# A new common order for 2,210 operations of a gated linear attention with a mixer behind it

## The chip, the cores and the metric

The kernel runs on one core of a Trainium2 chip. The metric is the device time of one execution in microseconds; the time before is 555.85 us, the median of 3 runs (555.32 to 556.29). The profile is one further execution taken by the hardware profiler, on core 0, whose span from the first to the last instruction is 552.8 us.

## The reference

The first half is a gated recurrence with complex gates per head (4 batches, 8 heads, 768 steps, 48 channels), the second a mixer on its result.

```python
scale = np.minimum(mag, 0.999) / (mag + 1e-06)
a_re_n, a_im_n = (a_re * scale, a_im * scale)
for t in range(S):
    new_re = ar * S_re - ai * S_im
    new_im = ar * S_im + ai * S_re
    S_re, S_im = (new_re + kv, new_im)
    y[:, :, t] = np.einsum('bhd,bhde->bhe', q[:, :, t], S_re)
...
h = xt @ U @ V
u = x + h.transpose(0, 2, 1)
ch = np.maximum(u @ w_ch1, 0.0) @ w_ch2
return (u + ch).astype(np.float32)
```

All arrays are float32 apart from the weights of the mixer, which arrive as float64 words and are narrowed on the chip.

## The kernel before, in words

**Tiles and stages.** A batch of 768 steps is cut into 6 chunks of 128, so there are 24 chunks; two chunks make a group (12 groups, for the gates) and two make a block of the mixer (12 blocks, m = 0 to 11). For a group, the gates are loaded (`load_a`), their magnitudes and logarithms are worked out on ScalarE and VectorE (`magnitudes_of`), summed along time by a matmul and exponentiated (`within`, tile `es`), and their angles are summed by a matmul and rounded (`angles`, tile `F`; L764 is VectorE's part, L758, L755 and L761 are the matmuls) and turned into cosine and sine (`waves_of`, tile `cs`). The decay over a whole chunk is the last row of `es`; it is stored to DRAM (`TD<-es`, L706) and loaded back turned (`T<-TD`, L709). For a chunk, q and k are loaded (L548) and v (L550), weighed by `es` and multiplied by `cs` on VectorE (`prep`, tile `QKC`), transposed on TensorE (L816) and copied by ScalarE (L822); then come the products inside the chunk (`inner`, L845), the state (`dk`, L865, and `G`), and the outputs (`y`, L894 and L902). The mixer runs over blocks: a low-rank mix (L960), a transpose (L976), the up product and the down product. Block 0 uses plain up products (L991); blocks from 2 on use products with fewer multiplications (`few`, L1103) and the down product in a Strassen-like form (`down_two`, L1235, whose sums on VectorE are L1227 and whose additions to the result are L444). For that form w2 is changed in place once, for block 1 (`w2_of(0, 1)` becomes a difference, L1305).

**Narrowing the weights.** w1 arrives in six loads and w2 in six more (`stage<-in_moe_w_ch_dram`, L569), each followed by five steps on VectorE, or three there and two on ScalarE (`single`, L582 to L588).

**The order.** The kernel does not issue its instructions where they are written. Every step is added to a `Plan` as a numbered operation with its engine, what it reads and what it writes. `ORDER` is a tuple of all 2,210 numbers: the operations are issued in this common order, and so each engine's own queue is the tuple filtered by engine (SyncE 192 operations, VectorE 793, ScalarE 553, TensorE 624, GpSimd 48). An engine works through its queue strictly in order: an operation that has to wait holds up everything behind it on the same engine. Reads and writes given to `add` are used in `Plan.order` alone, for an assertion that no operation comes before what it needs and that no buffer is taken too early; the real waits are put in from the tiles that the instructions touch. Buffers in PSUM are given out in the order of the tuple as well.

**Fillers.** `SPARE` says ahead of which operation how many extra products of the identity with itself are issued (`idle`, L1387 and L1383); they write the buffer that the operation is about to take, and nothing reads them.

**The range count.** At the end a count of gates outside the range of this method (`judge`, tiles `bad`, `least`, `flag`) decides whether a slow general path runs. All engines load the flag (L1395) after their last work of the main path.

**Forms on TensorE.** Its operations differ in how they divide the array: whole (up, few, down), in halves of rows (`inner`, `y` L902), in quarters (`dk`, `y` L894), in row strips that are transposed (`tr`, `mixed`), and the corrections of block 0.

Of the kernel before, what the change touches and what calls it, by code (L numbers as in the profile page):

```python
# [114 lines left out]
)  # L115

SPARE = {
    125: 2, 135: 10, 199: 14, 209: 1, 223: 5, 243: 2,
}

DUMP = None
# [195 lines left out]
def kernel(  # L317
# [19 lines left out]
    DM = H * D  # L337
# [580 lines left out]
    def mixer(m, ahead=False):  # L918
# [281 lines left out]
        def down_two():  # L1200
# [29 lines left out]
            def product(to, part, x, y, reads, first=True):  # L1230
# [6 lines left out]
                for half in range(2):  # L1237
                    PE(0.975, RM, lambda half=half: products(half), reads(half) + [("w2s", 0)],
                       [to + (part,), ("bank", to[1])], steps=KH)
# [215 lines left out]
```

## Time and profile before

| | us |
|---|---|
| median of the runs | 555.85 |
| span of the profiled execution | 552.8 |
| TensorE busy | 526.9 |
| VectorE busy | 432.8 |
| ScalarE busy | 317.8 |
| GpSimd busy | 32.2 |
| first matmul starts | 11.04 |
| last addition on VectorE starts | 548.02 |

An operation's row gives its start, its length, engine and line, what is written from what, and in brackets how long the engine had been idle and who ended that. Several operations of one kind in a row are merged. PEld is the loading of weights into the array, which overlaps the products. A "place" is an operation's position in its engine's own queue, counted from 0 in the tuple; it comes from the code and not from the trace. "Work ahead" of an operation is the time of all operations before it in its queue, without waits.

### The profile page before, as it was taken

What the parts mean: (1) busy time and instruction counts of PE and PEld (TensorE: products, weight loads), DVE (VectorE), ACT (ScalarE), POOL (GpSimd) and SP (SyncE); (2) the same over time, 40 slices, a digit from 0 to 9 for tenths busy, and PEclk for the clock granted to TensorE, in tenths of its full rate; (3) what the DMA queues carried; (4) which work ended last, traced back from release to release, by engine and by line L of the source; (5) the groups of instructions that cost most, each with busy time, mean ns of one, the idle gap of its engine ahead of it and who ended that gap; (6) DMA issues with size and microseconds to landing.
All of it is one profiled execution on the core that took longest, in us unless ns stands there. A gap on an engine that the chain in (4) does not pass through costs nothing.

```text
span 552.8 us, 16672 instructions
## 1 busy us (share of the span) xinstructions
PE 526.9 (95%) x7228; PEld 477.3 (86%) x7228; DVE 432.8 (78%) x828; ACT 317.8 (57%) x553; POOL 32.2 (6%) x61
## 2 busy tenths in 40 slices
PE   2899999999999999999999999999999999999996
PEld 1677776767999987999999998999999989999995
DVE  6899989999999987998787987786953635567352
ACT  6889999795597787567827956626512232110100
POOL 1000000001010000102001001002000000000000
PEclk9999999999999999999999999999999999999999
DMA  9988876523441354314513425003300000000001
GB/s 229 187 184 174 195 170 151 144 30 87 88 89 30 56 104 77 59 31 85 91 38 67 74 38 111 2 1 59 59 9 23 17 11 15 8 8 23 21 9 34
DMA packets 150688, 39.92 MB, mean 72 GB/s; under 512 B 145912, under 2 KB 147408, under 8 KB 150608
## 3 DMA queue, kind: packets, MB, share of 16 engines
q1 hardware_dynamic: 148400, 34.43, 31.2%
q0 software_dynamic: 2208, 4.35, 2.3%
q8 instruction: 59, 0.97, 0.7%
q14 instruction: 21, 0.17, 0.1%
HBM read 33.60 MB, written 4.76 MB: 69 GB/s over the span
## 4 chain that ended last, share of the span: by engine, by line
PE 73%; DVE 12%; ACT 4%; issue 2%; DMA 1%; POOL 0%; DVEq 0%; SPq 0%; ACTq 0%; POOLq 0%
PE down L1235 26%; PE few L1103 25%; PE tr L816 4%; PE dk L865 3%; PE inner L845 3%; PE y L902 3%; PE up L991 2%; PE y L894 2%; DVE xo L444 1%; ACT gate L438 1%; PE rank L937 1%; PE ph L755 1%; PE mixed L960 1%; PE uTp L976 1%; PE es ps L691 1%
## 5 line engine op out<-in xcount | busy, mean ns | idle before, releaser
L1111 ACT COPY h<-few 128x512 f32<-128x512 f32 x60 | 35.1, 585 | 87.3 <-PE few L1103 87.1
L1235 PE MATMUL down<-w,h 128*128 128x192 f32 x396 | 72.7, 330 | 0.9 <-DVE xo L444 0.7
L438 ACT ACTIVATE gate<-gate 128x768 f32<-128x768 f32 (+2 forms) x74 | 65.6, 900 | 9.2 <-DVE GS L750 3.8
L1235 PEld LDWEIGHTS down<-w,h 128*128 128x128 f32 x396 | 64.5, 190 | 3.7 <-issue 1.5
L822 ACT COPY QK<-tr 112x512 f32<-112x512 f32 x96 | 49.9, 596 | 17.8 <-PE tr L816 17.7
L444 DVE TENSOR_TENSOR xo<-down,xo 128x192 f32<-128x192 f32 (+1 forms) x79 | 29.9, 385 | 33.9 <-PE down L1235 33.4
L1115 DVE CUSTOM_DVE_ANT_1 h<-few,h 128x512 f32<-128x512 f32 x60 | 40.5, 686 | 15.7 <-PE few L1103 11.8
L1103 PE MATMUL few<-extra,w 128*128 128x128 f32 x400 | 50.9, 276 | 0.0
L1103 PEld LDWEIGHTS few<-extra,w 128*128 128x128 f32 x400 | 48.0, 192 | 0.1
L441 DVE TENSOR_TENSOR QKC<-qk,cs 128x768 f32<-128x768 f32 x48 | 44.4, 950 | 1.7 <-PE dk L865 1.3
L1235 PE MATMUL down<-stage 128*128 128x192 f32 x198 | 37.9, 330 | 0.4 <-DVE xo L444 0.4
L438 ACT ACTIVATE es<-es ps 128x384 f32<-128x384 f32 x48 | 20.1, 502 | 31.2 <-PE es ps L691 29.2
L444 DVE TENSOR_TENSOR h<-few,h 128x512 f32<-128x512 f32 x30 | 20.6, 688 | 20.4 <-ACT h L1111 12.1
L1179 POOL DMA_DIRECT2D out_dram<-xo x32 | 17.9, 558 | 313.8 <-DVE xo L444 297.7
L991 PE MATMUL up<-uT,w 128*128 128x256 f32 x144 | 34.5, 387 | 0.7 <-ACT uT L980 0.7
L1235 PEld LDWEIGHTS down<-stage 128*128 128x128 f32 x198 | 32.3, 190 | 1.7 <-DVE xo L444 1.0
L1103 PE MATMUL few<-gate,w 128*128 128x128 f32 x240 | 32.2, 278 | 0.4 <-DVE gate L1075 0.4
L435 ACT ACT_TABLE_LOAD x24 | 30.8, 1283 | 1.1 <-PEq L1439 0.7
L816 PEld LDWEIGHTS tr<-ident,QKC 64*112 64x112 f32 x768 | 24.2, 130 | 8.3 <-issue 3.6
L816 PE MATMUL tr<-ident,QKC 64*112 64x64 f32 x768 | 28.9, 221 | 2.4 <-DVE QKC L441 2.4
L991 PEld LDWEIGHTS up<-uT,w 128*128 128x128 f32 x144 | 26.4, 190 | 5.3 <-ACT uT L980 0.9
L1103 PEld LDWEIGHTS few<-gate,w 128*128 128x128 f32 x240 | 29.3, 192 | 0.8 <-PE uTp L976 0.6
(161 smaller groups left out, 1100.4 us busy)
## 6 DMA issues: line engine op xcount, KB each, us to landing
stage<-in_moe_w_ch_dram SPq DMA_DIRECT2D x12, 768.0 KB
gate<-in_a_im_dram SPq DMA_DIRECT2D x24, 192.0 KB
gate<-in_a_re_dram SPq DMA_DIRECT2D x24, 192.0 KB
VP<-in_v_dram SPq DMA_DIRECT2D x24, 192.0 KB
qk<-in_q_dram SPq DMA_DIRECT2D x24, 192.0 KB
qk<-in_k_dram SPq DMA_DIRECT2D x24, 192.0 KB
out_dram<-xo POOLq DMA_DIRECT2D x12, 192.0 KB, 2.2
out_dram<-xo POOLq DMA_DIRECT2D x20, 96.0 KB, 2.1
```

Of the source, the lines that this page charges most:

```text
L435: ACT(1.4, rank, lambda: nc.scalar.preload_act_table_set(name), writes=[TABLE])
L438: return nc.scalar.activation(out=o, in_=i, func=f, **kw)
L441: nc.vector.tensor_tensor(out=o, in0=a, in1=b, op=OP.mult)
L444: nc.vector.tensor_tensor(out=o, in0=a, in1=b, op=OP.add)
L816: nc.tensor.transpose(out=get(*ps[r])[0:DQ, h], in_=get(*qkc)[at, h].rearrange("p u d -> p (u d)")[:, 0:DQ], identity=ident[at, at], tile_ ...
L822: nc.scalar.copy(out=get(*QK)[:, u].rearrange("p (h t) -> p h t", t=CH)[:, :, r * HC:(r + 1) * HC], in_=get(*ps[r])[0:DQ])
L991: nc.tensor.matmul(out=get(*ps)[:, e], lhsT=w1[:, f, (ff + e) * 128:(ff + e + 1) * 128], rhs=get(*uT)[:, f], start=(f == 0), stop=(f == KD ...
L1103: nc.tensor.matmul(out=get(*ps)[:, q], lhsT=w()[:, q * 128:(q + 1) * 128], rhs=v[0](), start=(n == 0 and q == 0), stop=True, skip_group_ch ...
L1111: ACT(c_act(n3 * CH) - 0.045, RU, lambda i=i, k=k: nc.scalar.copy(out=at(i, k), in_=get(*ps)), [ps], [o])
L1115: DVE(c_dve(n3 * CH), RU, lambda i=i, k=k: nc.vector._custom_dve(dve_ops.TENSOR_ADD_SAT, out=at(i, k), in0=get(*ps), in1=at(i, k), s0=math ...
L1179: queue.dma_start(out=out[b, c * CH:(c + 1) * CH, lo:hi], in_=get("xo", i)[:, lo:hi])
L1235: nc.tensor.matmul(out=get(*to)[:, part], lhsT=x(j), rhs=y[:, j], start=(first and j == 0), stop=(j == KH - 1), skip_group_check=not first)
```

## The change

The tuple `ORDER` is replaced as a whole, with the same 2,210 numbers in another sequence. Four operations have other reads or writes, and one filler of 34 is left out, the one ahead of operation 209, a state product of chunk 0.

```diff
 ORDER = (
-    95, 93, 91, 0, 92, 94, 196, 150, 5, 96, 99, 11, 3, 100, 4, 151, 97, 152, 101, 98, 149, 112, 115, 194, 116, 106, 218, 113, 102, 195, 107, 114, 117,
...
-    2188, 2182, 2178, 2185, 2183, 2189, 2199, 2184, 2192, 2190, 2186, 2193, 2187, 2191, 2195, 2194, 2200, 2196, 2201, 2197, 2198, 2202, 2203,
+    91, 95, 93, 99, 96, 97, 98, 101, 102, 92, 94, 100, 112, 104, 115, 106, 0, 5, 103, 113, 114, 117, 118, 105, 116, 119, 120, 6, 121, 3, 109, 107,
...
+    2182, 2178, 2188, 2185, 2184, 2183, 2175, 2192, 2186, 2187, 2190, 2193, 2195, 2199, 2194, 2189, 2200, 2196, 2191, 2197, 2198, 2121, 2125, 2201,
+    2202, 2203, 1710,
 )
 SPARE = {
-    125: 2, 135: 10, 199: 14, 209: 1, 223: 5, 243: 2,
+    125: 2, 135: 10, 199: 14, 223: 5, 243: 2,
 }
...
-                                                                     in_=get(*y[1])[side(r, 1)]), [y[1] + (r,)], [xi + (r + 1,)])
+                                                                     in_=get(*y[1])[side(r, 1)]), [y[1]], [xi + (r + 1,)])
...
-                    PE(0.975, RM, lambda half=half: products(half), reads(half) + [("w2s", 0)],
+                    PE(0.975, RM, lambda half=half: products(half), reads(half) + [("w2s", 0), ("w2i", 0)],
...
-                DVE(c_dve(DH if y is not None else DM), R0, f, [ps + (part,)] + ([] if also is None else [ps + (also,)]),
+                DVE(c_dve(DH if y is not None else DM), R0, f, [ps + (part,), ("bank", ps[1])] + ([] if also is None else [ps + (also,)]),
...
-                                                                    op=OP.subtract), [("w2s", 0)], ALL_W2)
+                                                                    op=OP.subtract), [("w2s", 0)], ALL_W2 + [("w2i", 0)])
```

What the sequence becomes for the operations that matter below, as places in the engine's own queue:

| operation (number) | engine | place before | place after |
|---|---|---|---|
| load of w1's first block (5) | SyncE | 7 | 5 |
| load of v of chunk 0 (196) | SyncE | 5 | 15 |
| store of es(1), group 0's decay (129) | SyncE | 25 | 11 |
| loads T<-TD of group 0 (130, 131) | SyncE | 31, 32 | 26, 24 |
| stores of es(2), es(3) (173, 174) | SyncE | 36, 37 | 33, 30 |
| loads of q, k of chunk 2 (265, 266) | SyncE | 30, 29 | 34, 31 |
| stores of es(4), es(5) (339, 340) | SyncE | 55, 57 | 45, 48 |
| first widening step of w1 block 0 (6) | VectorE | 15 | 11 |
| gate product with a_im, chunk 0 (108) | VectorE | 9 | 18 |
| F of chunk 0 (137) | VectorE | 22 | 23 |
| w1 block 1, first four steps (12, 14, 13, 15) | VectorE | 20, 21, 18, 23 | 19, 20, 21, 22 |
| F of chunk 3 (187) | VectorE | 63 | 60 |
| weighing of q, k of chunk 2 (268) | VectorE | 49 | 62 |
| transposes of chunk 4's second half (369) | TensorE | 59 | 58 |
| up block (0, 8), second product (260) | TensorE | 53 | 61 |
| inner products of chunk 2 (277) | TensorE | 38 | 42 |
| product of the range count (2208) | TensorE | 439 | 589 |
| cast of the flag (2209) | VectorE | 610 | 780 |
| store of block 8's second half (1710) | GpSimd | 41 | 47 |

164 rows, old and new, of the table ORDER are left out of this document.

## The prediction

> **What bounds the kernel now.** I read the page first, then the busy time by stretch, then what TensorE waited for.
>
> ```profile
> span 552.8 us, 16672 instructions
> PE 526.9 (95%) x7228; PEld 477.3 (86%) x7228; DVE 432.8 (78%) x828; ACT 317.8 (57%) x553; POOL 32.2 (6%) x61
> ```
>
> ```profile
> 0.00:44.00 44.00, 29.32 (x463) 22.63 (x464) 37.96 (x77) 34.47 (x61) 2.17 (x14) 1.00 0.97 201
> 44.00:80.00 36.00, 33.97 (x651) 27.43 (x649) 35.97 (x58) 33.79 (x59) 0.00 (x0) 1.00 0.82 177
> 80.00:200.00 120.00, 118.96 (x1653) 99.60 (x1649) 113.17 (x200) 94.97 (x158) 8.37 (x12) 1.00 0.42 90
> 200.00:300.00 100.00, 97.85 (x1407) 91.39 (x1406) 86.40 (x171) 68.16 (x118) 7.70 (x12) 1.00 0.35 66
> 300.00:400.00 100.00, 99.43 (x1476) 94.04 (x1476) 81.63 (x164) 59.84 (x109) 7.42 (x11) 1.00 0.24 47
> 400.00:500.00 100.00, 99.83 (x1279) 95.58 (x1272) 53.16 (x110) 22.13 (x47) 3.82 (x7) 1.00 0.05 14
> 500.00:548.00 48.00, 47.57 (x338) 46.62 (x336) 24.16 (x51) 4.41 (x8) 2.69 (x5) 1.00 0.05 18
> ```
>
> The columns are the stretch, its length, then busy time of PE, PEld, DVE, ACT, POOL, the granted clock, the DMA share and GB/s. From 44 us on TensorE stands still for 2.03 + 1.04 + 2.15 + 0.57 + 0.17 + 0.43 = 6.4 us in all. No order of the same products can take more than that out of these 504 us. The other reserve lies before 44 us: 14.7 us of TensorE idle, and fillers that only pass time. VectorE is as full as TensorE up to 80 us (35.97 of 36), so the early part is a race of two engines: TensorE follows VectorE at a distance, and this distance is never caught up later, because afterwards TensorE has work without a break.
>
> ```profile
> 71.00 1.83 DVE L441 TENSOR_TENSOR QKC<-qk,cs 128x768 f32<-128x768 f32 x2
> 72.98 0.66 PE L816 MATMUL tr<-ident,QKC 64*112 64x64 f32 x16 [0.53 <-DVE QKC L441]
> 23.58 0.95 DVE L654 CUSTOM_DVE_ANT_0 GL<-gate 128x768 f32<-128x768 f32 x1
> 24.45 1.82 DVE L441 TENSOR_TENSOR QKC<-qk,cs 128x768 f32<-128x768 f32 x2
> ```
>
> The first two rows show the distance at work: the transposes of chunk 4's second half start 0.15 us after VectorE's product, having waited for it. The other two give the unit in which I count: an operation of 0.95 us takes 0.87 of its queue (23.58 to 24.45). Counted like this, start to next start where nothing waits, the old order has 64.4 us of VectorE work up to the end of that product and 44.6 us of TensorE work ahead of the transposes. So VectorE has lost 72.83 - 64.4 = 8.4 us up to there, TensorE 72.98 - 44.6 = 28.4, and the step demands a lag of 64.4 - 44.6 = 19.8 us. Over all TensorE steps of the old order the largest such lag is 20.0 (the second product of up block (0, 8), which needs w1's last block), and 8.4 + 20.0 is the 28.4 seen. Above this the end adds 28.4 to 35 us of loss, which is the 6.4 us of idle.
>
> **The change, part by part.** The four edits of reads and writes (whole `y[1]`, `("w2i", 0)`, `("bank", ...)`) add names to a list that is only asserted against the order; they emit no instruction, so 0 us. What runs is the new tuple.
>
> *VectorE's own loss, first 40 us.*
>
> ```profile
> 5.04 0.56 DVE L657 CUSTOM_DVE_ANT_0 low<-gate 128x384 f32<-128x384 f32 x1 [2.40 <-DMA gate<-in_a_re_dram]
> 11.66 0.56 DVE L444 TENSOR_TENSOR GL<-GL,gate 128x384 f32<-128x384 f32 x1 [0.46 <-ACT gate L438]
> 19.16 0.55 DVE L764 SCALAR_TENSOR_TENSOR F<-F,ph 128x384 f32<-128x384 f32 x1 [1.54 <-ACT F L438]
> 18.55 0.58 ACT L438 ACTIVATE F<-ph,magic 128x384 f32<-128x384 f32 x1 [0.59 <-PE ph L758]
> ```
>
> Of the 8.4 us lost, 5.04 is the first landing, which stays; 0.46 and 1.54 are two waits. The new queue puts the first widening step of w1 in front of the 11.66 operation, and all four steps of w1's block 1 plus the product `gate * a_im` of chunk 0 between it and the 19.16 one. These fill the 2.0 us. ScalarE's copy of `prefix_z` and its steps of chunk 0 shift too, so that by the same durations the F of chunk 0 is ready about 1.0 us sooner than 18.55 + 0.58. Walking through the new queues with the trace's durations, chunk 0's QKC starts at 22.6 and not 24.45, a gain of 1.85. But F of chunk 3 (old place 63, new 60) comes too early by some 1.1 us, as its phase sum follows on TensorE and ScalarE. So I take 0.75. Bounds: 0 (every gain waits elsewhere) and 2.0.
>
> *The lag.* In the new tuple the same transposes have 42.8 us of TensorE and 60.3 us of VectorE work ahead, a lag of 17.5; the largest of all steps is 18.2 (inner products of chunk 2). VectorE's deferred work is what changed: the second product of up block (0, 8) stands 8 places later, and the weighing of chunk 2's q and k 13 later. 20.0 - 18.2 = 1.8 us. Bounds: 0, where ScalarE or a transfer is met first, and 1.8. Together 2.55.
>
> *Changes of form.* TensorE's operations differ in how they split the array; where the form changes, the same work takes longer.
>
> ```profile
> 180.66 1.09 PE few L1103 x8
> 192.98 1.17 PE down L1235 x6
> 251.99 0.89 PE few L1103 x8
> 252.88 0.98 PE down L1235 x6
> ```
>
> These rows are of the chain of waits: alone among others of their kind 0.89 and 0.98, beside a step of another form 1.09 and 1.17, 0.2 more. The old order has 160 such changes, the new 150. By the most 10 x 0.2 = 2.0 us; but which forms meet changes also (from quarter to full fewer, from row to full more), and the sum of every step's usual time in its own neighbourhood is 512.4 us against 512.0. I take 0.4; bounds -0.5 (the mix costs more) and 2.0.
>
> *Tail.*
>
> ```profile
> 539.74 0.36 DVE L444 TENSOR_TENSOR xo<-down,xo 128x192 f32<-128x192 f32 x1 [0.62 <-PE down L1235]
> 540.48 0.35 DVE L444 TENSOR_TENSOR xo<-down,xo 128x192 f32<-128x192 f32 x1
> 540.89 1.24 PE L1235 MATMUL down<-stage 128*128 128x192 f32 x6 [0.21 <-DVE xo L444]
> L1377 DVE CAST flag<-bad ps x1: 136/136/136, 389.3 to 389.3; 1x1 int32<-1x1 f32 x1
> L1395 PEldq TENSOR_LOAD <-flag x1: 487/487/487, 544.9 to 544.9; - x1
> L1395 ACTq TENSOR_LOAD <-flag x1: 462/462/462, 526.5 to 526.5; - x1
> ```
>
> The last 14 TensorE steps are the same in both. On VectorE a sum of h (0.47) no longer stands between the two additions at 539.74 and 540.48, so the 0.21 us of waiting goes, with some of the change of form beside it: 0.3, bounds 0 and 0.4. The flag is not made earlier but later: its cast moves from VectorE's place 610 to 780 of 793, near 534 us. ScalarE reads the flag once its own work is done, at 526.5, and would wait, but nothing is queued behind it; TensorE reads at 544.9, 10 us later than the cast. So 0.
>
> *The filler* left out is these two:
>
> ```profile
> 26.04 0.46 PE L1387 MATMUL dk<-ident 128*128 128x96 f32 x2
> ```
>
> It lies where TensorE waits for VectorE anyway: 0, and 0.4 at most if that cover went.
>
> *From 80 us on* I keep the remaining 4.4 us of idle (1.04 + 2.15 + 0.57 + 0.17 + 0.43). The trace shows no wait of the new order; bounds are 2.4 less, as the lag that steps near 200 us demand falls from some 7 to 8 us to 4 to 5 in the new tuple, and 4 more.
>
> Sum: 0.75 + 1.8 + 0.4 + 0.3 = 3.25 us. The profiled span is 552.8 and the median of the runs 555.85, 3.05 outside the span; I leave that as it is: span 549.6, median 552.6.
>
> **The rivals.**
>
> *SyncE's queue gets in the way: slower.*
>
> ```profile
> 15.38 2.02 SPq L548 DMA_DIRECT2D qk<-in_k_dram  x2
> 24.61 0.38 SPq L706 DMA_DIRECT2D TD<-es  x1
> 27.02 1.00 SPq L548 DMA_DIRECT2D qk<-in_q_dram  x1
> 28.13 5.41 SPq L709 DMA_DIRECT2D T<-TD  x2
> 22.71 0.95 DVE L441 TENSOR_TENSOR qk<-qk,es 128x768 f32<-128x768 f32 x1
> 37.38 0.95 DVE L441 TENSOR_TENSOR qk<-qk,es 128x768 f32<-128x768 f32 x1
> ```
>
> SyncE waits in order. The store of es(1) moves from place 25 to 11, ahead of chunk 0's and 1's q and k; group 1's stores move to places 30 and 33, around chunk 2's. Chunk 0's k was through at 17.40 and used at 22.71, so a load needs 5.3 us at most. In the new queue es(1) is ready near 14, when SyncE gets there, and costs about 1; chunk 2's last half goes out near 36.5 instead of 27.02, behind es(3), and VectorE wants it near 44.9 (place 62, no longer 37.38). 36.5 + 1 + 5.3 = 42.8: 2.1 us to spare. If the slow pair T<-TD (5.41) comes in between, it is 3.3 late, VectorE stands, and TensorE with it. The same pattern returns at group 2 (stores at places 45 and 48 ahead of q and k of chunk 5). One such hit takes back the whole gain, two give 552.6 + 6.6 = 559.2. It decides once chunk 2's last half is issued after 44.9 - 5.3 = 39.6. Against it: after 80 us all but three of the new queue's loads have over 6 us of TensorE work between what releases them and what uses them.
>
> *The gain is hidden anyway: no change.* The idle of 2.15 us at 200 to 300 shows that something else sets TensorE's pace there. If TensorE, being earlier, waits that much more: 2.55 of 3.25 lost, 555.2. For it: VectorE lost time for TensorE there as well (86.40 of 100). Against: the smaller lags named above.
>
> *More gain.* The later idle shrinks by the 2.4 of the bounds and VectorE's 2.0 come whole: 552.6 - 2.4 - 1.2 = 549.0.
>
> *A colder start.*
>
> ```profile
> 11.04 1.62 PE L695 MATMUL es ps<-GL,prefix_r 128*128 128x384 f32 x2 [11.04 <-DVE GL L444]
> 13.30 1.49 PE L695 MATMUL es ps<-GL,prefix_r 128*128 128x384 f32 x2
> 33.93 0.91 PE L695 MATMUL es ps<-GL,prefix_r 128*128 128x384 f32 x2
> ```
>
> The first two pairs take 0.6 to 0.7 us more than a later one. If the steps to 20 us (three of this size) stayed that slow because TensorE begins about 1 us sooner, that is 3 x 0.65 = 2.0: 554.6. [...]
>
> **How the numbers follow.** Forecast 0.52, more gain 0.17, slower by the queue 0.19, no change 0.09, colder start 0.03. A run of this kernel tells 0.2% (1.1 us) from no change: faster is below 554.7, slower above 557.0. Faster is 0.52 + 0.17 + half of the colder start = 0.70; same 0.09 + the other half = 0.11; slower 0.19. Predicted is 552.6. The largest gains together are 2.0 + 1.8 + 2.0 + 0.4 + 2.4 = 8.6, 547.3; that all come at once is unlikely, so the range begins at 547.8. With no gain early, 0.5 lost on forms and 4 more of idle it would be 552.6 + 2.55 + 0.9 + 4 = 560.0; the range ends at 557.6, between one hit and two of the queue, and leaves the rest out. The forecast's own range is 550.5 to 554.3.
>
> **What would show it.** Right: chunk 0's QKC on VectorE near 22.6; the first transposes near 23.6 instead of 25.45; chunk 4's, after 42.8 us of work and 25.9 of loss, near 68.7; about 2.5 us less TensorE loss at 80 us, and TensorE idle from 80 us on still near 4.4; no 0.21 in the tail. Wrong: VectorE waiting for a transfer of q or k before 60 us, T<-TD in front of it on SyncE; or TensorE idle over 7 us after 80 us; or products longer by more changes of form.

## The result, and the profile after

The changed kernel takes 548.01 us (median of 4 runs, 547.12 to 550.12) against 556.07 us for the kernel before in the same comparison: ratio 0.986, 95% interval 0.9838 to 0.9883. That is 8.1 us less, where 3.25 were forecast. The profiled execution spans 545.8 us, 7.0 less than the one of before.

The first lines of the page of the changed kernel, and its busy time by the stretches that were shown of before (stretch, length, then PE, PEld, DVE, ACT, POOL, granted clock, DMA share, GB/s):

```profile
span 545.8 us, 16645 instructions
PE 522.9 (96%) x7226; PEld 475.8 (87%) x7226; DVE 433.5 (79%) x828; ACT 316.2 (58%) x553; POOL 31.9 (6%) x61
```

```profile
0.00:44.00 44.00, 29.30 (x464) 22.92 (x465) 38.84 (x79) 36.16 (x64) 2.03 (x14) 1.00 0.87 184
44.00:80.00 36.00, 33.26 (x647) 27.05 (x646) 32.99 (x49) 33.60 (x59) 0.00 (x0) 1.00 0.80 180
80.00:200.00 120.00, 119.56 (x1666) 100.01 (x1665) 115.27 (x200) 95.15 (x156) 7.88 (x11) 0.99 0.46 95
200.00:300.00 100.00, 99.94 (x1456) 94.43 (x1454) 88.23 (x173) 65.86 (x116) 7.60 (x12) 1.00 0.32 61
300.00:400.00 100.00, 100.00 (x1431) 95.36 (x1430) 77.94 (x153) 57.02 (x102) 7.58 (x12) 1.00 0.27 50
400.00:500.00 100.00, 100.00 (x1284) 95.78 (x1283) 58.89 (x129) 24.95 (x53) 3.56 (x7) 1.00 0.06 15
500.00:541.00 41.00, 40.86 (x291) 40.27 (x289) 21.09 (x50) 3.51 (x6) 3.21 (x6) 1.00 0.07 24
```

TensorE's idle time behind 44 us is 2.74 + 0.44 + 0.06 + 0 + 0 + 0.14 = 3.4 us, 3.0 less than before. From 80 us on it has almost gone (0.64 against 4.4); from 44 to 80 us it has grown by 0.7. TensorE's busy time over the whole execution fell too, from 526.9 to 522.9 us, with the same products but for one filler of less than 0.5 us.

Idle time alone therefore does not show where the time went. TensorE runs the same 624 steps in both kernels, and at some points of its queue exactly the same set of steps is done in both traces. The time at which the next step starts can be compared there without any model:

| steps done | before, us | changed, us | difference |
|---|---|---|---|
| 6 | 26.43 | 24.80 | -1.63 |
| 28 | 45.03 | 43.65 | -1.38 |
| 43 | 59.05 | 58.12 | -0.93 |
| 83 | 91.42 | 91.88 | +0.47 |
| 117 | 129.54 | 130.17 | +0.63 |
| 187 | 187.44 | 187.22 | -0.22 |
| 289 | 268.13 | 265.72 | -2.41 |
| 324 | 296.28 | 292.40 | -3.87 |
| 590 | 515.17 | 508.61 | -6.56 |
| 616 | 539.54 | 532.89 | -6.65 |
| 623 | 546.84 | 539.72 | -7.12 |

So an early lead of about 1 us is won, lost again between 59 and 92 us, and the whole gain is made from 130 us on, bit by bit: 0.85 to 187 us, 2.2 to 268, 1.5 to 296, 2.7 to 515, and 0.6 behind that.

What eats the early lead stands in TensorE's rows around 78 us:

```profile
22.93 1.82 DVE L442 TENSOR_TENSOR QKC<-qk,cs 128x768 f32<-128x768 f32 x2
23.94 0.66 PE L817 MATMUL tr<-ident,QKC 64*112 64x64 f32 x16 [0.78 <-DVE QKC L442]
69.92 1.12 PE L817 MATMUL tr<-ident,QKC 64*112 64x64 f32 x32 [0.61 <-DVE QKC L442]
74.80 2.36 PE L866 MATMUL dk<-VP,QKC 64*64 64x48 f32 x96
77.09 1.15 PE L846 MATMUL inner<-QK 112*64 112x64 f32 x31
80.01 1.98 PE L846 MATMUL inner<-QK 112*64 112x64 f32 x33 [1.77 <-issue]
81.92 0.87 PE L938 MATMUL rank<-xo,UV 128*32 128x384 f32 x4
```

```profile
76.50:80.00 3.50, 1.74 (x54) 1.55 (x50) 1.76 (x4) 3.50 (x6) 0.00 (x0) 1.00 0.71 205
80.00:83.40 3.40, 3.39 (x45) 2.04 (x44) 2.54 (x4) 2.56 (x4) 0.00 (x0) 0.50 0.02 5
83.40:87.00 3.60, 3.60 (x135) 3.44 (x132) 3.50 (x6) 1.35 (x3) 0.00 (x0) 1.00 0.31 46
```

The first transposes come at 23.94 and not 25.45, those of chunk 4 at 69.92 and not 72.98. Then follow 96 products of the state (two passes of 48) and the inner products of chunks 4 and 5 without a long operation in between, and in the middle of the inner products TensorE stands still for 1.77 us. This standstill is called the hole below. "issue" says that TensorE waited for nothing that the profile shows. In the window behind this hole the granted clock (the eighth column) is 0.50: the 33 inner products take 1.98 us there, and the rank products behind them 1.44 instead of 0.78 to their next step. Compared with the same steps at full clock (the loads experiment below) the half clock costs 0.83 + 0.66 = 1.5 us, the hole 1.77.

Instructions come to the core by DMA too. The page lists their queue with packets, MB and share of 16 engines:

```profile
q8 instruction: 59, 0.97, 0.8%
```

0.97 MB in 59 packets is 16,384 bytes each, and the trace has the time of every packet. TensorE's 14,551 instructions (products, weight loads and the few that only wait) make 247 for each of the 59 packets. In the changed kernel one of these packets lands from 68.33 to 69.70 us, the next only from 77.64 to 78.61, after 439 TensorE instructions; TensorE resumes 1.40 us after its end.

### The profile page after: what moved, and what is told of

The parts are those of the page before. It is cut to its first block, busy times and chain, and to the rows that moved or that the text cites. A ratio compares the mean times of both kernels' runs of the same rounds, so it can differ in the third digit from the quotient of the medians.

```text
span 545.8 us, 16645 instructions
## 1 busy us (share of the span) xinstructions
PE 522.9 (96%) x7226; PEld 475.8 (87%) x7226; DVE 433.5 (79%) x828; ACT 316.2 (58%) x553; POOL 31.9 (6%) x61
## 3 DMA queue, kind: packets, MB, share of 16 engines
q0 software_dynamic: 2208, 4.35, 2.4%
## 4 chain that ended last, share of the span: by engine, by line
PE 87%; DVE 5%; ACT 3%; DMA 2%; issue 1%; SPq 1%; DVEq 0%; ACTq 0%
PE down L1236 29%; PE few L1104 25%; PE inner L846 4%; PE up L992 4%; PE tr L817 4%; PE dk L866 4%; PE y L903 4%; PE y L895 2%; DMA gate<-in_a_im_dram 2%; PE rank L938 2%; PE mixed L961 2%; PE uTp L977 1%; PE es ps L692 1%; ACT gate L439 1%; PE ph L756 1%
## 5 line engine op out<-in xcount | busy, mean ns | idle before, releaser
L823 ACT COPY QK<-tr 112x512 f32<-112x512 f32 x96 | 51.1, 595 | 34.8 <-PE tr L817 34.6
L742 POOL DMA_DIRECT2D gate<-F x15 | 12.2, 810 | 324.3 <-DVE F L765 170.6
L817 PE MATMUL tr<-ident,QKC 64*112 64x64 f32 x768 | 27.4, 219 | 2.9 <-DVE QKC L442 2.9
L1180 POOL DMA_DIRECT2D out_dram<-xo x32 | 20.2, 681 | 168.1 <-issue 86.1
```

The lines of the kernel that those rows point to most:

```text
L817: nc.tensor.transpose(out=get(*ps[r])[0:DQ, h], in_=get(*qkc)[at, h].rearrange("p u d -> p (u d)")[:, 0:DQ], identity=ident[at, at], tile_ ...
L823: nc.scalar.copy(out=get(*QK)[:, u].rearrange("p (h t) -> p h t", t=CH)[:, :, r * HC:(r + 1) * HC], in_=get(*ps[r])[0:DQ])
```

## The experiments

Two things had to be settled: where the gain is made, and what the hole is. Theory A said that the gain is made behind 130 us and the early lead is given back; theory B that the early lead is the cause and the later waits vanish because of it. Theory F said that the hole is TensorE waiting for its own instructions; theory G that it is a hidden wait for another engine. Further theories are named in the expectations. Ratios are to the kernel before, run beside each experiment (medians 555.3 to 556.3 us). Where a diff lists a few numbers, it is a piece of one engine's queue. A "seam" is where a run goes over from one sequence to the other.

### One part of the order at a time

The first run has the new sequence early and the old one late, the second the reverse, cut after 600 numbers.

```diff
 ORDER = (
-    (before) all 2210 numbers in the old sequence
+    the first 600 of the new sequence, the others as in the old one
```

> The first 600 numbers of the new tuple (up to about 130 us of TensorE's work, with the filler left out), then all others in the old sequence. Theory A (the gain is made behind 130 us, where the new queues leave TensorE almost no waits; what is won before 80 us is given back by 100 us): ratio to the kernel before 0.996 to 1.003, TensorE idle behind 130 us near the old 4 us. Theory B (the early lead is the gain, and because TensorE and VectorE are in better step the later waits vanish of themselves): ratio 0.986 to 0.990, TensorE idle behind 130 us near 0.5 us.

564.93 us, ratio 1.0153 (1.0124 to 1.0182): slower by 8.7 us, which neither theory had. The hole at 78 us was there (2.80 us, half clock behind it), and at the seam TensorE stood for 1.54 us, waiting for ScalarE, and for 4.54, waiting for VectorE, with 6.8 us at half clock behind that. These take more than any early lead could give, so the run tells little of theory B.

```diff
 ORDER = (
-    (before) all 2210 numbers in the old sequence
+    the first 600 of the old sequence, the others as in the new one
```

> The first 600 numbers of the old tuple, then all others in the new sequence, the filler kept. Theory A (the gain is made behind 130 us): ratio 0.986 to 0.990, TensorE idle behind 130 us below 1 us. Theory B (the early lead is the gain): ratio 0.997 to 1.002.

549.94 us, ratio 0.991 (0.9879 to 0.9941): 6.3 us less without any of the new early order. Behind 200 us TensorE's idle time is 0.3 us (0.2 in the changed kernel). The seam cost 0.78 us at 139, and a hole of 1.67 us stood at 198; with these two the ratio is just above the range of theory A, and far from that of theory B.

The first run was repeated with the cut at one time on all engines (what the changed kernel's trace starts before 115 us).

```diff
 ORDER = (
-    the first 600 of the new sequence, the others as in the old one
+    what the new order starts before 115 us, the others as in the old one
```

> The new sequence for all operations that the changed kernel's trace starts before 115 us, the old sequence for all others (the seam is at one time on all engines, which it was not in the first run of this kind). Theory A (early gain of 1 to 3 us, given back by the hole at 78 us and the half clock behind it): ratio 0.999 to 1.006. Theory B (the early lead lets the later waits vanish): ratio 0.986 to 0.991. If the hole stays away by chance: ratio 0.993 to 0.998.

560.55 us, ratio 1.0096 (1.0078 to 1.0115). Again slower, outside all three ranges. The profiled execution is the longest of the seven (566.93 us), so its trace shows more than the median lost: the hole of 2.58 us at 77 us with 13.6 us at half clock behind it, and at 134 us a wait of 3.61 us for VectorE, with 6.8 us more at half clock:

```profile
137.32 0.69 PE L756 MATMUL ph<-GS,prefix_r 128*128 128x384 f32 x1 [3.61 <-DVE GS L750]
```

At 120 us VectorE has worked 108.6 us in the changed kernel's trace and 110.0 in that of before, so it comes later to the seam than the old queues behind it expect. What decides against theory B is the stretch behind the seam: the run is 11.8 us behind the kernel before after 125 steps and 12.1 at the end, and the first run 9.8 after 140 steps and 9.9 at the end. The old late queues gain nothing there. And in the changed kernel itself no lead is left after 83 steps, ahead of the whole gain.

Two further runs measured the late part. The first changes the order only for what the old one starts from 288 us on, the second is the late part of above with the last correction of the loads (below), which takes most of the hole at 198 us away.

```diff
 ORDER = (
-    (before) all 2210 numbers in the old sequence
+    what the old order starts before 288 us, the others as in the new one
```

> The old order for all operations that the trace of before starts until 288 us, the new sequence for all others. Theory S (the late gain comes bit by bit, wherever the new queues of all engines leave TensorE slack): behind 288 us the old order loses some 5.5 us to TensorE's rate and the new one 2.5, so 2 to 3.5 us less: ratio 0.9935 to 0.9965. Theory T (the gain needs the state that the new order has built up before 288 us): less than 1 us, ratio 0.998 to 1.002.

552.75 us, ratio 0.9938 (0.9915 to 0.9962). In its trace TensorE is 1.66 us behind the kernel before after 312 steps (a half clock at 26 to 30 us, which the trace of before does not have) and 1.59 ahead at the end: 3.25 us gained behind 288 us, as theory S expected.

> The first 600 numbers of the old tuple as in e2_late_new, then the sequence of e13_loads3, so without the hole of 1.7 us that e2_late_new had at 198 us. Theory A (the gain is made behind 130 us): ratio 0.986 to 0.990, 1 to 2 us less than e2_late_new, and what e13_loads3 has beyond that is the early part without its hole, 2 to 4 us. If the early part is worth nothing even without its hole, e13_loads3 and this run are within 1 us.

549.39 us, ratio 0.9887 (0.9863 to 0.9911). Theory A holds in its main point; the hole at 198 us shrank to 0.90 us only. The second half of the expectation missed: the run with the corrected loads and the new early part (543.52 us, below) is 5.9 us faster than this one, where 2 to 4 were expected. So the early part is worth something once its hole is smaller: in the traces that run is 2.9 us ahead of this one after 105 steps, 3.9 after 136 (behind the seam), 5.0 after 208 (behind the hole) and 6.4 at the end. Why the last 1.4 us come is open.

A count shows what the late part has that the old one lacks. For every TensorE step the traces give the time between the end of the last operation of another engine that it needs (an input, or the emptying of its bank of PSUM) and its own start. Steps with less than 0.3 us (how inputs and banks are counted moves an entry by up to 2):

| stretch, us | before | changed | new only behind 288 us |
|---|---|---|---|
| 200 to 300 | 23 | 11 | 23 |
| 300 to 400 | 26 | 15 | 16 |
| 400 to 500 | 23 | 11 | 11 |
| 500 to end | 8 | 3 | 3 |

There are some 80 of these tight steps in the old order and some 40 in the new one. The run with the new order behind 288 us has the old count ahead of it and the new one behind it. An estimate from the two traces says how much of the gain they carry. The usual time from one step's start to the next is the median over the same pair of kinds of step, both with more than 0.5 us to spare, behind 80 us in both traces. Behind 130 us the intervals that begin or end with a tight step exceed it by 6.9 us in the old order and by 1.7 in the new one, which is 5.2 of some 7 us gained there; all other intervals exceed it by 3.4 and 1.4. No run took the tight steps out by themselves, so this is worked out and not tested.

### Can single waits be taken out of the old order?

If the late waits are local, moving a few operations of ScalarE forward should do. Theory L says that they are; theory H says that the next wait takes their place. Here are the rows of before, at 198 us, that the first move was made for:

```profile
197.63 1.12 PE L845 MATMUL inner<-QK 112*64 112x64 f32 x32
198.04 1.49 ACT L438 ACTIVATE gate<-gate 128x1536 f32<-128x1536 f32 x1 [1.07 <-DVE GS L750]
199.56 0.64 ACT L913 COPY xo<-y 64x192 f32<-64x192 f32 x2
200.22 0.32 ACT L911 COPY xo<-y 128x192 f32<-128x192 f32 x1
200.86 0.78 PE L865 MATMUL dk<-VP,QKC 64*48 64x48 f32 x21 [0.47 <-issue]
```

The three copies empty two banks; their data was there at 197.80. They stand behind a gate step of 1.49 us which itself had waited 1.07 for VectorE, so the second bank was free only at 200.54. The move took TensorE's 0.7 us at 200.86 for a wait for it (0.47 of them show as idle; the rest lies in products that the trace books as busy). The program and the trace say otherwise. The steps that take these two banks start at 202.51 and 205.04, long after. The idle time lies inside a step, behind 11 of its 16 products, where no wait for another engine stands, and it ends 1.50 us after an instruction packet (198.39 to 199.36). It is a smaller hole of the kind at 78 us.

```diff
 ORDER = (
-    1178, 836, 837, 835,
+    837, 1178, 836, 835,
...
-    1817, 1476,
+    1476, 1817,
...
-    646, 455,
+    455, 646,
...
-    406, 405, 407,
+    407, 406, 405,
```

> The old order with ten operations of ScalarE at other places of its queue and nothing else changed: the copies 836, 837, 835 ahead of the gate step 1178, the activation 1476 ahead of the gate step 1817, 455 ahead of the gate step 646, 407 ahead of 406. Theory L (the old order's waits behind 80 us are local, each a small operation of ScalarE or VectorE that frees a bank and stands behind a long one, and TensorE sets the pace): the waits of 0.70, 0.68, 0.59 and 0.52 us vanish and the time falls by 1.2 to 2.5 us, ratio 0.9945 to 0.998. Theory H (something else sets the pace there, so that the next wait takes it up): ratio 0.998 to 1.002.

556.1 us, ratio 1.0016 (1.0005 to 1.0028). Of the three copies only one (837) came ahead of the gate step, other than the expectation says. TensorE's queue is the same in both, so the two traces can be subtracted step by step. At 200 us 0.85 us are won, after 0.61 had been lost just before: TensorE waits for ScalarE there (0.31 us of it idle), comes later to the end of its instruction block, and the hole is gone. That tells nothing of a wait for a bank. At 344 us 0.44 are won and 0.83 + 0.64 lost: the gate step 1817 now waits for 1476 and ends at 345.55 instead of 343.51, and the copies of chunk 19 and an addition of VectorE, which TensorE needs, stand behind it. Only 0.44 of the loss comes back in the 200 us that follow. At this place the wait is real, as theory L has it, and the next one takes its place, as theory H has it.

```diff
 ORDER = (
-    1817, 1476, 1794, 1793, 1797, 1798,
+    1476, 1794, 1793, 1797, 1798, 1817,
...
-    1178, 836, 837, 835,
+    837, 1178, 836, 835,
...
-    406, 405, 407,
+    407, 406, 405,
... (VectorE)
-    1818, 1819, 1481,
+    1481, 1818, 1819,
```

> The old order with the gate step 1817 behind the copies of chunk 19 and 1476 (instead of only 1476 ahead of it), the copies 836, 837, 835 ahead of the gate step 1178, and 407 ahead of 406. TensorE's queue is that of before. Theory L (local waits on a TensorE that sets the pace): the waits at 344 us (0.44 and 0.68) and 200 us (0.70, of which 0.56 came back in the earlier run) vanish, 1 to 1.5 us less behind 80 us: ratio 0.997 to 0.999. Theory H (the next wait takes it up): no step down that lasts, ratio 0.999 to 1.002.

560.65 us, ratio 1.0098 (1.0073 to 1.0123): worse still. Again only 837 of the three copies came ahead of the gate step, and one addition of VectorE (1481) moved too. The rows of this run at 344 us show the chain:

```profile
345.62 1.52 ACT L438 ACTIVATE gate<-gate 128x1536 f32<-128x1536 f32 x1
347.17 0.96 DVE L654 CUSTOM_DVE_ANT_0 GL<-gate 128x768 f32<-128x768 f32 x1 [1.74 <-ACT gate L438]
349.04 1.48 DVE L444 TENSOR_TENSOR xo<-mixed,xo 128x384 f32<-128x384 f32 x3
349.74 0.73 PE L976 MATMUL uTp<-ident,xo 128*128 128x128 f32 x3 [3.51 <-DVE xo L444]
```

The gate step, moved behind the copies, ends at 347.14; VectorE's next operation needs it, and the additions that TensorE waits for stand behind that one: 3.51 us. So neither of these two attempts to mend a queue of the old order helped; that none could is not shown. The whole late queue of one engine, or of two of TensorE, VectorE, ScalarE and SyncE, cannot be taken over: by what the operations read and write, the queues would wait for each other in a circle. Of the sets of three, TensorE, VectorE and ScalarE together would not; that was not tried.

### What the hole at 78 us is

The first test moves the boundaries of TensorE's instruction blocks: 24 more fillers ahead of its first product.

```diff
 SPARE = {
-    125: 2, 135: 10, 199: 14, 223: 5, 243: 2,
+    109: 24, 125: 2, 135: 10, 199: 14, 223: 5, 243: 2,
```

> The changed kernel with 24 more fillers ahead of TensorE's first product, where it stands idle anyway; all later TensorE instructions stand 96 places further on in its stream. Theory F (the 1.8 us hole of TensorE before 80 us, in the inner products of chunk 4 and 5, which no engine releases, is a late fetch of TensorE's own instructions, 256 of them at a time): the hole is gone from that operation or smaller than 0.5 us there, and the time falls by up to 1.8 us if no new one opens elsewhere: ratio 0.982 to 0.987. Theory G (the hole is a wait for another engine that the trace does not show): the hole of 1.8 us stays at the same operation, ratio 0.985 to 0.988. If the fillers also speed up the first products by 0.6 us each, the first transposes come up to 1 us earlier under both.

550.33 us, ratio 0.9884 (0.985 to 0.9918). In the profiled execution (span 543.0 us) there is no hole there: 96 state products and 64 inner products run through. Smaller ones stand elsewhere, 0.93 us at 70 us in the transposes and 0.66 at 193.

```profile
75.17 2.06 PE L866 MATMUL dk<-VP,QKC 64*64 64x48 f32 x96
77.16 2.09 PE L846 MATMUL inner<-QK 112*64 112x64 f32 x64
```

But only two of the six executions are like that (544.8 and 545.4 us at a mean granted clock of 1.00); four have 550.1 to 550.8 us at 0.992 to 0.994. Their lower clock fits a hole with a half clock behind it, but only the one execution has a trace. A wait that the order fixes would be there each time, which speaks against G.

The filler of the change, put back, is the next smaller shift.

```diff
 SPARE = {
-    125: 2, 135: 10, 199: 14, 223: 5, 243: 2,
+    125: 2, 135: 10, 199: 14, 209: 1, 223: 5, 243: 2,
```

> The changed kernel with the one filler ahead of operation 209 put back. By the prediction it costs 0 to 0.4 us: ratio to the kernel before 0.986 to 0.988, the same as the changed kernel. If the time differs by more than 1 us, the filler (four more instructions on TensorE) did something else than fill a wait.

549.79 us, ratio 0.987 (0.9843 to 0.9897): the filler itself is worth nothing that can be measured. The hole was there, with 3.08 us and 6.8 us of half clock.

Next, a long operation between the small products.

```diff
 ORDER = (
-    372, 397, 408,
+    408, 372, 397,
...
-    926, 571,
+    571, 926,
```

> The changed kernel with two of TensorE's long operations moved: the first rank product (408, 8 products in 1.4 us) in between the small products of chunks 4 and 5, ahead of the inner products 372, and one down product (571, 6 products in 1.2 us) ahead of the inner products 926. Theory F (TensorE runs out of its own instructions where small products follow each other, because they use up 512 instructions before the next 256 have landed): the hole at 78 us falls from 1.8 us (3.1 in the run with the filler) to below 0.5 us, the half clock behind it does not come, ratio to the kernel before 0.978 to 0.984. Theory G (a hidden wait of the inner products of chunk 4 for another engine): the hole stays at 372, ratio 0.985 to 0.989.

547.0 us, ratio 0.9859 (0.9828 to 0.9889), not below 0.984, and the hole was still in step 372, 0.6 us later. By what was written ahead of it, this run speaks for theory G:

```profile
77.12 0.85 PE L938 MATMUL rank<-xo,UV 128*32 128x384 f32 x8
77.91 0.91 PE L846 MATMUL inner<-QK 112*64 112x64 f32 x23
80.28 1.39 PE L846 MATMUL inner<-QK 112*64 112x64 f32 x41 [1.46 <-issue]
```

The instruction packet started at 77.64, just as in the changed kernel, and TensorE resumed at 80.28: the end of the hole is set by the packet and not by TensorE. The expectation under theory F missed because the delay of the packet (over 2 us) was larger than the time given (0.8 us). The 512 instructions of that expectation are two blocks of 256, which in the changed kernel's trace TensorE begins from 67.75 us up to the hole at 78.24; the packet behind the hole has landed at 78.61. How many TensorE can hold no run shows. And the hole now stands behind 23 of the 32 products of step 372, where it stood behind 31: 8 products sooner, with the 8 rank products moved ahead of it, so after the same number of TensorE's instructions. A wait for another engine would have stayed at its product. The hole of 1.46 us had no half clock behind it.

The decisive test leaves TensorE's queue alone and moves traffic.

```diff
 ORDER = (
-    387, 687, 688, 342, 27, 58, 25, 712, 64, 26, 711,
+    387, 342, 27, 58, 25, 64, 687, 688, 712, 26, 711,
```

> The changed kernel with three loads on SyncE (q and k of chunk 6, half of chunk 7; 576 KB) moved behind the load of w2's fourth block, from about 70 us to 85 us; they are used at 94 and 97 us. TensorE's queue is that of the changed kernel. Theory F with traffic (the fetch of TensorE's instructions comes late because the DMA engines are full from 69 to 78 us): the fetch starts at least 1 us sooner, the hole at 78 us falls below 0.8 us and the half clock does not come: ratio 0.978 to 0.985. If the traffic does not delay the fetch: the same hole of 1.8 us or more and the half clock, ratio 0.985 to 0.989.

547.87 us, ratio 0.9858 (0.9838 to 0.9879), no faster than the changed kernel, but the trace shows two separate things:

```profile
76.31 2.31 PE L846 MATMUL inner<-QK 112*64 112x64 f32 x64
87.86 0.59 PE L961 MATMUL mixed<-r,V 64*128 64x192 f32 x2
90.31 0.72 PE L961 MATMUL mixed<-r,V 64*128 64x192 f32 x5 [1.86 <-issue]
```

The hole at 78 us is gone. The packet of instructions lands from 74.96 us on, 2.7 us sooner (TensorE itself is 0.8 us earlier there), with a DMA share of 0.54 from 72 to 76.5 us (1.01 in the changed kernel), and the mixing product 447 starts at 87.86 us instead of 91.88. There it waits 1.86 us, for V: its third piece (26) stood behind the loads I had moved and went out at 86.14 us. A half clock followed from 92.3 to 95.7 us, and the gain was gone again: 4.0 us ahead of the changed kernel after 83 steps, 0.1 after 89. So the next run has V ahead:

```diff
 ORDER = (
-    387, 342, 27, 58, 25, 64, 687, 688, 712, 26, 711,
+    387, 342, 27, 58, 25, 26, 64, 687, 688, 712, 711,
```

> The changed kernel with nine places of SyncE's queue changed and nothing else: the three loads of q and k (chunk 6, half of chunk 7) behind w2's fourth block as in the run before, and V's third piece (26) ahead of it, so that the mixing product 447 need not wait for V. Theory F with traffic: no hole at 78 us, no wait of 1.9 us at 88 us, no half clock at 80 or 92 us, about 3.5 us less than the changed kernel: span 541.5 to 543.5, ratio to the kernel before 0.976 to 0.982. If something else gives the gain back, so that TensorE is slowed again before 120 us: ratio 0.984 to 0.988.

545.91 us, ratio 0.9808 (0.9785 to 0.9832). The hole at 78 us is 1.09 us without a half clock, and one of 1.51 us stands at 196 us, where again chunk products follow each other (10 and 11). The expected span was 541.5 to 543.5; it is 544.3, with these two holes in it. The same edit at 196 us:

```diff
 ORDER = (
-    1225, 1175, 1174, 865, 1226, 1250, 1227, 867, 1249,
+    1175, 1174, 865, 867, 1225, 1226, 1250, 1249, 1227,
```

> The kernel of e9_loads2 with one more group of loads moved on SyncE: q and k of chunks 12 and 13 and v of chunk 12 (960 KB) behind the load 867, which waits for its own store, so from about 190 us to 195 us; they are used from 199 us on. Theory F with traffic: the fetch that came at 194.4 us comes at least 1 us sooner and the hole of 1.5 us at 196 us falls below 0.7 us; up to 1.5 us less than e9_loads2: ratio to the kernel before 0.977 to 0.981. If the traffic does not delay the fetch: the hole stays, ratio 0.980 to 0.983.

543.52 us (542.83 to 544.01), ratio 0.9781 (0.9759 to 0.9804): 4.5 us faster than the changed kernel, by 18 places of SyncE's queue alone. The packet came at 192.44 us, 2 us sooner, and the hole at 196 us is gone. This version beats both kernels.

```profile
span 541.7 us, 16644 instructions
44.00:80.00 36.00, 34.51 (x688) 27.97 (x686) 34.18 (x52) 35.27 (x61) 0.00 (x0) 1.00 0.71 166
80.00:200.00 120.00, 119.90 (x1730) 101.31 (x1728) 116.91 (x204) 96.67 (x158) 7.89 (x11) 1.00 0.50 99
200.00:300.00 100.00, 100.00 (x1415) 95.04 (x1411) 86.86 (x170) 65.72 (x118) 7.62 (x12) 1.00 0.34 66
```

```profile
76.07 1.15 PE L846 MATMUL inner<-QK 112*64 112x64 f32 x31
78.36 1.16 PE L846 MATMUL inner<-QK 112*64 112x64 f32 x33 [1.14 <-issue]
```

After 83 steps it is 2.59 us ahead of the kernel before (the changed one 0.47 behind), after 117 steps 2.40, at the end 11.0. The last 1.14 us at 78 us remain.

One run joined the loads of e9_loads2, the move of 571 and the 24 fillers.

> The loads of the run above, the down product 571 ahead of the inner products 926 (the other place where TensorE ran dry, near 198 us) and the 24 fillers ahead of TensorE's first product. Theory F: 0.5 us less than the run above from the warm start and up to 0.5 from the hole at 198 us: ratio 0.975 to 0.981. If the shifted instruction stream opens a hole elsewhere: 0.981 to 0.987.

547.32 us, ratio 0.9838 (0.981 to 0.9866). As in the second case of the expectation, a new hole opens: with the fillers the boundary falls into the state products, and the half clock stands behind it:

```profile
73.78 1.37 PE L866 MATMUL dk<-VP,QKC 64*64 64x48 f32 x63
77.09 0.67 PE L866 MATMUL dk<-VP,QKC 64*48 64x48 f32 x17 [1.93 <-issue]
```

The table has the holes of this kind over 0.8 us in all traces, and the three of the kernel before, each with the packet that ends it (times from the traces' records of the instruction queue and of the granted clock):

| run | hole, us | packet, us | resumes after its end | half clock behind it, us |
|---|---|---|---|---|
| changed kernel | 78.24 to 80.01 | 77.64 to 78.61 | 1.40 | 3.4 |
| e1_early_new | 77.62 to 80.42 | 77.84 to 79.07 | 1.35 | 3.4 |
| e3_filler_back | 78.03 to 81.11 | 78.70 to 79.84 | 1.27 | 6.8 |
| e8_early_new2 | 77.20 to 79.78 | 77.09 to 78.46 | 1.32 | 13.6 |
| e10_best | 75.16 to 77.09 | 74.43 to 75.68 | 1.41 | 3.4 |
| e2_late_new | 198.50 to 200.17 | 197.43 to 198.61 | 1.56 | none |
| e9_loads2 | 195.53 to 197.04 | 194.44 to 195.74 | 1.30 | none |
| e5_spread | 78.82 to 80.28 | 77.64 to 78.89 | 1.39 | none |
| e3_filler_back | 199.60 to 200.75 | 198.02 to 199.07 | 1.68 | none |
| e13_loads3 | 77.22 to 78.36 | 75.87 to 77.14 | 1.22 | none |
| e9_loads2 | 77.88 to 78.97 | 76.26 to 77.53 | 1.44 | none |
| e14_late288 | 273.75 to 274.71 | 271.99 to 273.14 | 1.57 | none |
| e4_pad | 70.16 to 71.09 | 68.28 to 69.67 | 1.42 | none |
| e15_late_loads3 | 198.43 to 199.33 | 196.97 to 197.90 | 1.43 | none |
| e6_loads | 197.90 to 198.71 | 196.02 to 197.03 | 1.68 | none |
| before | 138.21 to 138.51 | 136.19 to 137.12 | 1.39 | none |
| before | 200.39 to 200.86 | 198.39 to 199.36 | 1.50 | none |
| before | 272.62 to 273.06 | 270.56 to 271.68 | 1.38 | none |

In every case TensorE resumes 1.2 to 1.7 us after an instruction packet ends, whatever the operation is. The count of TensorE's instructions settles it. In the 17 traces TensorE stands for over 0.25 us behind 44 us 107 times. In 26 cases, among them all of the table, the instruction behind the gap has the same remainder when TensorE's instructions are counted in 256s (193 stand ahead of it). The other 81 are spread over 34 remainders, and each of them has a wait for a semaphore ahead of it. So theory F holds, in the old order too, only with smaller holes.

### The range count by itself

```diff
 ORDER = (
-    2204, 2205, 2206, 2207, 2208, 2209 where the old order has them
+    2204 ahead of 1905, 2205 and 2206 ahead of 2049, 2207 ahead of 2035, 2208 ahead of 2118, 2209 ahead of 2178
```

> The old order with only the range count's six operations (2204 to 2209) where the new order has them, between the same neighbours behind them. By the prediction 0: the flag is cast near 540 us and read by TensorE at 544.9. Ratio 0.999 to 1.001. If an operation of the count stood in the way of TensorE in its old place, up to 0.5 us less.

555.56 us, ratio 1.0 (0.9987 to 1.0013). Its place costs and brings nothing.

## Why the forecast had the direction right and the place of the gain wrong

The forecast was 2.55 us gained early, 0 behind 80 us, 0.4 on forms and 0.3 in the tail. The compared steps give 0.63 lost up to 117 steps, 7.28 gained from there to the tail and 0.47 in the tail, 7.1 in all. That the direction came out right is in good part luck: the early terms that carried most of it gave nothing in this kernel, and the one put at 0 gave nearly the whole gain.

**VectorE's own loss: right.** Chunk 0's QKC was forecast for 22.6 us and came at 22.93; the first transposes for 23.6, and came at 23.94. The walk gave 1.85 us, the trace 1.52, and 0.93 are left after 43 steps, where 0.75 was taken for what the later wait leaves.

**The lag: lost in this kernel.** Chunk 4's transposes came at 69.92, not near 68.7: behind the same 42.8 us of work TensorE has lost 27.1 us, where 25.9 were forecast and 28.4 stood before. After 83 steps the changed kernel stands 0.47 us behind. Without the hole (1.77) and the half clock (1.5) it would be 2.8 ahead there, where 0.75 + 1.8 = 2.55 were forecast. The run with corrected loads is 2.59 ahead after 83 steps, but it is another order of loads with a hole of 1.14 us of its own, so that this is nearly the forecast is partly chance. The forecast had no term for the hole, and a slower TensorE was thought of for the start only, not for the half clock from 80.0 to 83.4 us.

**From 80 us on: the step that failed.** It was "I keep the remaining 4.4 us of idle", with 2.4 less as the bound, though the smaller lags of the new tuple near 200 us had been seen. The compared steps give 0.63 + 6.65 = 7.3 us there, from 117 steps on to the tail, and the runs show that the new late sequence alone brings most of it (549.94 us with the old early part, 3.25 us from 288 us on). Two things were wrong in the term. The idle columns were read as all that waits cost ("No order of the same products can take more than that"): the gap of 0.7 us at 200 us shows as 0.47, and TensorE's booked busy time fell by 4.0 us. (Of the idle time of before, 0.30 + 0.47 + 0.44 us are holes in which TensorE waits for instructions; the changed kernel has one of 0.33 us left there, at 198.) And the term was kept at zero because the trace of before cannot show the new order's waits, when the same walk through the new queues that gave the early terms could have been made for the late ones.

**Changes of form: of the wrong sign, by a working from the traces.** With each step's usual time beside the same neighbours, taken from both traces, the new sequence of forms behind 80 us costs 457.3 us and the old 455.8: 1.5 more, where 0.4 less was taken. This was not tested on its own.

**Tail:** 0.47 (7.12 - 6.65), forecast 0.3. The 0.21 us of waiting is gone:

```profile
532.89 2.12 PE L1236 MATMUL down<-stage 128*128 128x192 f32 x12
534.85 1.14 PE L1236 MATMUL down<-stage,more 128*128 128x192 f32 x6
```

**Filler and count:** nothing that can be measured, as forecast. The flag is cast at 530.0 us (forecast near 534).

**The rivals.** SyncE's queue did not get in the way: the last half of chunk 2 goes out at 35.89 us, much as worked out (36.5) and ahead of 39.6, and VectorE weighs it without a wait:

```profile
35.89 1.03 SPq L549 DMA_DIRECT2D qk<-in_q_dram  x2
44.78 0.95 DVE L442 TENSOR_TENSOR qk<-qk,es 128x768 f32<-128x768 f32 x1
```

What the loads did was another thing: close together, from 69 to 75 us, they held up TensorE's instructions: with three of them moved, the packet came 2.7 us sooner (TensorE itself 0.8). "More gain", 549.0, names what came true, the later idle, at a third of its size, and comes within 1 us of the measured time only because the early gain that it also counts on was lost. The gain was not hidden between 200 and 300 us. The start was no colder: in both traces the full clock begins at 15.1 us. With the 24 fillers, which bring it at 7.0, the first pair takes 0.88 us instead of 1.62, and TensorE is 0.5 us earlier at 19 us.

## What to carry to other kernels

Idle time of the bounding engine is not the most that another order can gain: compare traces at points where the same steps are done, and count the steps whose last input came only tenths of a microsecond before them. When a hand-made order is changed, walk every stage of it with the durations of the trace, not only the crowded one. And when loads are drawn together, look at what runs beside them: here TensorE's own instructions came by DMA too, in 59 packets of 16,384 bytes, and loads that were not due (q and k, 23 us ahead of their use) belonged elsewhere: with them moved, the packet behind the hole at 78 us came 2.7 us sooner. When an engine stands without a wait, count its instructions: here 26 of 107 gaps stood behind the same count up to multiples of 256, whatever the operation, and those of the table ended 1.2 to 1.7 us after an instruction packet, so they were no waits for another engine. And mending a single place of a tight order can make the next one late, as it did twice here.

## What the runs showed of the chip that was not expected

TensorE ran out of instructions. They come in packets of 16,384 bytes, and in all 17 traces no block of 256 instructions is begun sooner than 1.2 us after its packet has landed. In the changed kernel TensorE went through one block of small products in 3.44 us (74.80 to 78.24), and the next packet started 2.8 us after that block was begun, where the median of this trace is 0.45. In the table the holes of 1.4 us and more stand behind blocks during which the DMA share was 0.85 to 1.10. Smaller holes stand behind such a share too (0.44 us at 1.06, before, 272 us), and also behind 0.21 (0.30 us, before, 138 us) and 0.53 (1.14 us, e13_loads3). So full DMA engines go with the largest holes here, but are not needed for one. Most of the 59 packets cost no such hole: behind 44 us the changed kernel has two of over 0.25 us (1.77 and 0.33), the kernel before three (0.30, 0.47 and 0.44).

The clock fell after short holes. In the traces here, behind 44 us, idle times of TensorE of 1.77 us and more were followed by half clock, those of 1.67 us and less were not, and the half clock lasted 3.4, 6.8 or 13.6 us.
